# Decoding the weights on VectorE alone, reciprocals as a broadcast weight, the seam's hash ahead of its stage

## The chip, the cores and the metric

The kernel runs on one core of a Trainium2 chip. The metric is the device time of one execution in microseconds. The engines are TensorE (PE, with its weight loads PEld), VectorE (DVE), ScalarE (ACT), GpSimd (POOL) and SyncE (SP), which issues most of the DMAs. Each engine works off its own queue in order; semaphores order them against each other.

## The reference, cut to what matters

```python
# q, k, v: (4, 8, 768, 64) f32; proj: (64, 6)
q_bucket = sum(((q @ proj) > 0) * 2**arange(6)); k_bucket likewise
mask   = q_bucket[:, :, :, None] == k_bucket[:, :, None, :]
scores = where(mask, (q @ k.T) / 8, -1e9); scores -= scores.max(-1)
attn   = exp(scores); attn /= attn.sum(-1) + 1e-9
x      = (attn @ v) as (batch, 768, 512)
h      = relu(x @ w_in)                       # (768, 1024) per batch
gate   = sigmoid(conv3 along the sequence of h with conv_w)
out    = (h * gate) @ w_out                   # (768, 512) per batch
```

The three weights of the second part arrive as 64-bit floats. Each is made on the chip into two parts, high and low, that TensorE can multiply.

## The kernel before, in words

**Units.** Two heads of a batch are a pair; there are 16 pairs. A unit is one head's 128 query rows against all 768 keys; a pair has 12 units, and 192 units are counted through by `i` in the main loop. For unit `i` the loop issues, in this order: the products (line 286, four matmuls into PSUM tile `s`), the maximum (line 299, VectorE, which also moves `s` to `e` in SBUF), the transposes of unit `i-3` (line 329, six) and their copy to `at` (line 336, ScalarE), and the exponential of unit `i` (line 306, ScalarE). `s`, `t` and the hash share a ring of three PSUM tiles, so TensorE can be about one unit ahead of VectorE.

**Bursts.** Two row blocks of two heads, four units, are one step of the values. In every fourth unit (`i` = 3, 7, 11, ...) TensorE gets a block of 14 more matmuls: two that spread the reciprocals of the sums (line 350, transposes of `rec`), and twelve that multiply by `v` (line 355). This unit is called a burst here. In the next one ScalarE copies the spread factors to `rs`; in the next burst VectorE multiplies by them (line 364), and GpSimd splits the product into `xh` and `xl` (lines 365, 366). This holds for the first six pairs. The later ones (`late`, from pair 6 on) divide `e` itself on GpSimd (line 314).

**Decoding.** Lines 87 to 140 decode 16 blocks of weights, 128x512 each: the size of the upper word on ScalarE (87), a clamp on GpSimd (90), four operations on VectorE (95, 97, 102, 104), a cast on ScalarE (136) and two operations on GpSimd (139, 140). This is a generator, `split_weights`, in which the stages of successive blocks overlap. From unit 7 on each burst moves it by `RATE` = 3.75 steps (line 527), a step being mostly one VectorE operation; the feed-forward stage moves it by two steps an iteration. The cast waits for the block's last VectorE operation, since the result lies where the raw block lay.

**The next pair.** Its rows `R` (q and k of two heads, 768 KB) are loaded in the pair before the last (line 191, issued by SP in the pair's unit 7, once nothing reads `R` any more). In units 1 to 7 of a pair the generator `prepare` (line 231) makes the next pair's operands: split of the first head (`hi`, line 204, and in place the rest, line 209), hash (line 219: matmuls of `R` with the projections; line 222: bits on VectorE; 224: their weights on GpSimd), split of the second head. Each part is moved to its partitions by DMAs of SP: 192 KB moves of `hi` and `R`, eight small ones of the bits.

**Stages.** After the first units of pairs 6, 10 and 14 and at the end comes the feed-forward stage of a batch, `ffn`: 16 column blocks through `hidden` (lines 393 to 412) and `output` (423). The place where the loop enters it, in the third unit of a pair, is called the seam. At the seam `prepare` has made two of its seven steps; the rest, the hash among them, come in iterations 3 to 7 of the stage.

Of the kernel before, what the change touches and what calls it, by code (L numbers as in the profile page):

```python
# [28 lines left out]
F32_MAX = 2.0 ** 127 * (2.0 - 2.0 ** -23)  # L29
# [9 lines left out]
RATE = 3.75  # L39
# [4 lines left out]
def lsh_attention_conv_ffn(ctx, tc, qk, v, hw, w_in, conv_w, w_out, consts, ident_in, out):  # L44
# [23 lines left out]

    Q2s = [cp.tile([96, 2, S], F32R, name=f"q2_{i}") for i in range(2)]
# [4 lines left out]
    class Decode:  # L74
# [4 lines left out]
        def __init__(self, raw, n, name):  # L79
            pr, self.name = raw.rearrange("p (n two) -> p n two", two=2), name  # L80
            self.lo, self.hi = pr[:, :, 0].bitcast(U32), pr[:, :, 1]
            self.up, self.low = (ring(wp, bufs, [P, WC], I32, f"w{x}", f"w{x}{name}")[:, :n]
                                for x, bufs in (("u", 2), ("l", 5)))
# [15 lines left out]

        def lower(self):  # L100
            V, up, low = nc.vector, self.up, self.low
# [3 lines left out]
            yield  # L105

    def split_weights():

        todo, ends = [], None

        def ahead():
            if fetched:
                raw, name = fetched.pop(0)
                todo.append(Decode(raw, WC, name))
                todo[-1].size()

        ahead()  # L120
        ahead()
        yield
        for d in todo:
            d.clamp()
        yield
        while todo:
            d = todo.pop(0)
            ahead()
            yield from d.upper()
            if ends:  # L130
                ends()
            if len(todo) == 2:
                todo[-1].clamp()
            yield from d.lower()
            blk = weights[d.name] = cp.tile([P, 2, WC], F32R, tag=f"w{d.name}", name=f"w{d.name}")
            nc.scalar.copy(blk[:, 0, :], d.upf)

            def ends(d=d, blk=blk):
# [38 lines left out]
    class Pair:  # L177
# [53 lines left out]
        def prepare(self):  # L231

            sa, sb, hs = self.split(0), self.split(1), self.hash()
            for now in ((sa,), (), (hs, sa), (hs,), (sb,), (), (sb,)):
                for g in now:
                    next(g, None)
# [362 lines left out]
```

## Time and profile before

| | |
|---|---|
| time, three runs | 748.12, 752.3, 996.83 us; median 752.3 |
| the profiled execution | 750.76 us |
| its span, first to last instruction | 749.0 us |
| mean granted clock of TensorE | 0.984 of full speed |
| PE busy | 714.4 us (95%) |
| DVE busy | 499.2 us (67%) |
| ACT busy | 509.2 us (68%) |
| POOL busy | 373.6 us (50%) |
| share of PE in the chain that ended last | 69% |

The run of 996.83 us stands far from the two others. Busy shares are means over stages with different limits; the stages lie at 0 to 205 us (pairs 0 to 5 and the decoding), 205 to 278 (first feed-forward stage), then 105 us of attention, a stage of some 70 us, and so on. Clock shares are of 2.4 GHz; the lower level is 1.2 GHz.

### The profile page before, as it was taken

The page shows a single profiled execution, that of the slowest core. Times are in us where ns is not written, and L with a number is a line of the kernel's source. Part 1 is how long each engine was busy: PE and PEld are TensorE (multiplying, and loading weights), DVE is VectorE, ACT ScalarE, POOL GpSimd, SP SyncE. Part 2 cuts the span into 40 slices and gives each one's busy share as a digit, 9 for nine tenths or more (in the row PEclk, how much of TensorE's full clock was granted, in tenths as well). Part 3 has the DMA queues.
Part 4 walks back from the last instruction along what each step waited for, and adds up shares of the span by engine and source line. Part 5 has one row for each costly group of instructions (what it writes and reads, how often), then busy time and mean ns, then how long its engine had stood idle before and what let it go on. Part 6 is the DMA issues. An engine that isn't in the chain of part 4 may idle for free.

```text
span 749.0 us, 13385 instructions
## 1 busy us (share of the span) xinstructions
PE 714.4 (95%) x4588; PEld 587.5 (78%) x4588; DVE 499.2 (67%) x1195; ACT 509.2 (68%) x954; POOL 373.6 (50%) x372
## 2 busy tenths in 40 slices
PE   5989999988899999999999999999999999999997
PEld 3767777776679987777788988777788897778986
DVE  7588999977667656666657655665666665564663
ACT  5867887886655548778774557787785547785554
POOL 4366777756566324755735423656645323341221
PEclk8999999998999999999999999999999999999999
DMA  3876576553412102365441302255461211000011
GB/s 141 198 204 155 141 206 181 168 162 85 114 43 72 64 37 70 82 181 136 121 121 31 104 1 105 68 150 132 119 163 33 70 43 63 2 1 1 0 43 43
DMA packets 30357, 72.18 MB, mean 96 GB/s; under 512 B 5937, under 2 KB 7505, under 8 KB 30289
## 3 DMA queue, kind: packets, MB, share of 16 engines
q1 hardware_dynamic: 27696, 62.88, 30.9%
q10 hardware_dynamic: 2592, 8.44, 3.6%
q8 instruction: 37, 0.61, 0.3%
q14 instruction: 32, 0.25, 0.1%
HBM read 27.40 MB, written 6.29 MB: 45 GB/s over the span
## 4 chain that ended last, share of the span: by engine, by line
PE 69%; DVE 4%; POOL 4%; DMA 3%; ACT 1%; issue 1%; SPq 0%; POOLq 0%; DVEq 0%
PE o L423 18%; PE h L393 17%; PE s L286 11%; PE t L329 11%; PE v L355 11%; DVE e L299 2%; DMA k<-R 1%; DMA R<-in_qk 1%; PE hash L219 1%; POOL wuo L139 1%; POOL e L314 1%; POOL wo L140 1%; ACT e L306 1%; DVE wuo L97 1%; POOL R L209 1%
## 5 line engine op out<-in xcount | busy, mean ns | idle before, releaser
L299 DVE TENSOR_SCALAR_CACHE_REDUCE e<-s 128x768 f32<-128x768 f32 x192 | 183.3, 955 | 80.9 <-PE s L286 72.1
L306 ACT ACTIVATE e<-e,st 128x768 f32<-128x768 f32 x192 | 181.2, 944 | 23.1 <-DVE st L303 12.8
L336 ACT COPY at<-t 128x768 f32<-128x768 f32 x192 | 152.3, 794 | 47.3 <-PE t L329 47.1
L329 PE MATMUL t<-ident,e 128*128 128x128 f32 x1152 | 164.5, 280 | 19.9 <-DVE e L299 17.9
L314 POOL TENSOR_SCALAR e<-e,st 128x768 f32<-128x768 f32 x120 | 109.3, 911 | 117.3 <-ACT at L336 59.9
L329 PEld LDWEIGHTS t<-ident,e 128*128 128x128 f32 x1152 | 133.4, 144 | 42.6 <-DVE e L299 22.4
L402 DVE SCALAR_TENSOR_TENSOR ht<-ht,cw 128x384 f32<-128x384 f32 (+1 forms) x128 | 117.8, 921 | 70.0 <-ACT ht L400 66.8
L412 POOL TENSOR_TENSOR g<-ht,g 128x384 fp32r<-128x384 f32 x64 | 72.0, 1125 | 163.9 <-ACT g L411 129.7
L423 PE MATMUL o<-wo,g 128*128 128x512 f32 x576 | 143.3, 395 | 0.7 <-POOL g L412 0.7
L393 PE MATMUL h<-xh,wi 128*128 128x386 f32 x512 | 142.0, 340 | 0.0
L355 PE MATMUL v<-at,v 128*64 128x256 f32 x1152 | 134.9, 383 | 0.0
L423 PEld LDWEIGHTS o<-wo,g 128*128 128x128 f32 x576 | 107.0, 188 | 23.5 <-ACT ht L400 1.2
L286 PE MATMUL s<-K,Q 128*128 128x384 f32 x384 | 118.7, 391 | 1.0 <-POOL K L253 0.9
L355 PEld LDWEIGHTS v<-at,v 128*64 128x64 f32 x1152 | 78.7, 137 | 45.5 <-issue 10.9
L286 PE MATMUL s<-k,q 96*128 96x384 f32 x384 | 102.2, 348 | 2.2 <-DVE e L299 2.2
L405 ACT ACTIVATE ht<-ht 128x384 f32<-128x384 f32 x64 | 33.6, 525 | 96.4 <-DVE ht L402 96.4
L393 PEld LDWEIGHTS h<-xh,wi 128*128 128x128 f32 x512 | 94.0, 188 | 3.7 <-ACT ht L400 1.2
L393 PE MATMUL h<-xl,wi 128*128 128x386 f32 x256 | 86.8, 339 | 0.0
L286 PEld LDWEIGHTS s<-K,Q 128*128 128x128 f32 x384 | 60.1, 196 | 22.2 <-issue 17.4
L286 PEld LDWEIGHTS s<-k,q 96*128 96x128 f32 x384 | 72.9, 197 | 3.0 <-ACT q L266 3.0
L406 DVE TENSOR_TENSOR ht<-ht 128x384 f32<-128x384 f32 x64 | 41.5, 649 | 31.5 <-ACT ht L405 31.3
L209 POOL TENSOR_TENSOR R<-R,hi 128x768 fp32r<-128x768 f32 x30 | 60.4, 2014 | 0.9 <-PE hash L219 0.8
(75 smaller groups left out, 622.2 us busy)
## 6 DMA issues: line engine op xcount, KB each, us to landing
R<-in_qk SPq DMA_DIRECT2D x15, 768.0 KB
K<-hi SPq DMA_DIRECT2D x60, 192.0 KB
v<-in_v SPq DMA_DIRECT2D x16, 384.0 KB
out<-osb SPq DMA_DIRECT2D x24, 256.0 KB
Q<-hi SPq DMA_DIRECT2D x30, 192.0 KB
q<-hi SPq DMA_DIRECT2D x30, 192.0 KB
Q<-R SPq DMA_DIRECT2D x30, 192.0 KB
k<-R SPq DMA_DIRECT2D x30, 192.0 KB
```

The costliest lines, as they stand in the source:

```text
L209: nc.gpsimd.tensor_tensor(lo, R, hi.bitcast(F32), ALU.subtract)
L286: nc.tensor.matmul(self.sp[:, half, :HS], A[:, h, qs], C[:, h, half * HS:(half + 1) * HS], start=(kk == 0), stop=(kk == 1))
L299: nc.vector.tensor_scalar(self.e.rearrange("p (a b) -> p a b", a=2), self.sp[:, :, :HS], MASKED, None, ALU.max, ALU.max, accum_out=self.st ...
L306: nc.scalar.activation(self.e, self.e, AF.Exp, bias=self.st[:, 1:2], scale=SCALE, accum_out=self.sum)
L314: nc.gpsimd.tensor_scalar(self.e, self.e, self.st[:, 3:4], 0.0, ALU.mult, ALU.add)
L329: nc.tensor.transpose(self.tp[:, c // 3, c % 3 * P:(c % 3 + 1) * P], self.e[:, c * P:(c + 1) * P], ident)
L336: nc.scalar.copy(pr.at[self.h][:, :, :, self.tq * P:(self.tq + 1) * P], self.tp[:, :, :3 * P].rearrange("p j (c q) -> p j c q", c=3))
L355: nc.tensor.matmul(av[h * D:(h + 1) * D, :QB], vt[:, c, h, :], ats[h][:, c // 3, c % 3, :], start=(c == 0), stop=(c == NCK - 1), tile_posi ...
L393: nc.tensor.matmul(hp[:, :HW], w, x[:, c0:c0 + HW], start=(n == 0), stop=(n == 3 * NCC - 1))
L402: nc.vector.scalar_tensor_tensor(t[:, a:z], ht[:, o + k - 1 + a:o + k - 1 + z], cw[:, f, k:k + 1], t[:, a:z], ALU.mult, ALU.add)
L412: nc.gpsimd.tensor_tensor(g[:, 1, :], t, g[:, 0, :].bitcast(F32), ALU.subtract)
L423: nc.tensor.matmul(op, l, r, start=(f == 0 and n == 0), stop=(f == NFC - 1 and n == 2))
```

## The change

- **Decoding.** ScalarE's size and GpSimd's clamp go. VectorE does a bitwise and, a maximum, and the old four operations, six in a row, then ScalarE's cast and GpSimd's two operations follow at once; blocks no longer overlap in the generator. `RATE` is 6, less one in a pair's unit 3. Nothing is decoded in the feed-forward stages. `low` and `up` share one ring of four buffers with `bits` and `osb`.
- **Sums.** Three fixed tiles hold 1e-9 in every second column, written once; the exponential's sum goes into the other, and a `tensor_reduce` adds both. The reciprocals are spread on TensorE: four matmuls whose weight is one column, read 64 times, against the identity. GpSimd's spread (line 323) goes.
- **Order.** The product with the factors is made in place in `rs` (two buffers). GpSimd's split of it comes after the decoding of the burst. `prepare` is two generators: the hash in units 3 and 4 ahead of the values, and the splits behind the decoding. In the four units before a seam the hash's generator is moved twice a unit.

```diff
-RATE = 3.75
+RATE = 6.0
+    sums4 = [cp.tile([P, 2 * QB // P, 2], F32, name=f"sums{i}") for i in range(3)]
+    for t in sums4:
+        nc.gpsimd.memset(t, 1e-9)
...
-        def size(self):
-            nc.scalar.activation(self.lowf, self.hi.bitcast(F32), AF.Abs)
-        def clamp(self):
-            nc.gpsimd.tensor_scalar(self.lowf, self.lowf, F32_MAX, F64_MIN, ALU.min, ALU.max)
-        def upper(self):
+        def vector(self):
             V, up, low = nc.vector, self.up, self.low
+            V.tensor_scalar(low, self.hi, 0x7FFFFFFF, None, ALU.bitwise_and)
+            yield
+            V.tensor_scalar(self.lowf, self.lowf, F64_MIN, None, ALU.max)
+            yield
             V.tensor_scalar(low, low, 3, 0x3FFFFFFF, ALU.logical_shift_left, ALU.bitwise_and)
             yield
             V.scalar_tensor_tensor(up, self.hi, -0x40000000, low, ALU.bitwise_and, ALU.bitwise_or)
             yield
...
+        while fetched:
+            raw, name = fetched.pop(0)
+            d = Decode(raw, WC, name)
+            yield from d.vector()
+            blk = weights[name] = cp.tile([P, 2, WC], F32R, tag=f"w{name}", name=f"w{name}")
             nc.scalar.copy(blk[:, 0, :], d.upf)
+            nc.gpsimd.tensor_tensor(d.upf, d.upf, blk[:, 0, :].bitcast(F32), ALU.subtract)
+            nc.gpsimd.tensor_tensor(blk[:, 1, :], d.upf, d.lowf, ALU.add)
+            yield
...
-            for now in ((sa,), (), (hs, sa), (hs,), (sb,), (), (sb,)):
+            return steps((None, None, hs, hs)), steps((sa, None, sa, None, sb, None, sb))
...
-            nc.vector.tensor_scalar(sums, sums, 1e-9, None, ALU.add)
-            nc.vector.reciprocal(sums, sums)
-            nc.gpsimd.tensor_scalar(pr.rec, sums.unsqueeze(3).to_broadcast([P, QB // P, 2, D]), 1.0, 0.0,
-                                    ALU.mult, ALU.add)
+            nc.vector.tensor_reduce(pr.inv, self.sums, mybir.AxisListType.X, ALU.add)
+            nc.vector.reciprocal(pr.inv, pr.inv)
...
-                nc.tensor.transpose(av[:, QB + t * P:QB + (t + 1) * P],
-                                    rec[:, t].rearrange("p h d -> p (h d)"), ident)
+                for h in range(2):
+                    nc.tensor.matmul(av[h * D:(h + 1) * D, QB + t * P:QB + (t + 1) * P],
+                                     inv[:, 2 * t + h:2 * t + h + 1].to_broadcast([P, D]), ident,
+                                     start=True, stop=True, tile_position=(0, h * D))
...
-            fetch(1)
             background(1)
             if i >= 3:
-                next(prep[0], None)
+                prepare(0)
+                prepare(1)
...
-            background(1)
...
-        next(prep[0], None)
+        prepare(0)
+        if ending:
+            prepare(0)
         for _ in range(1 + NCK if ending else AVS[(i - LAG) % 4]):
...
         if burst and i >= W0:
-            background(RATE)
+            background(RATE - (k == PREP + 2))
+        for last in parts:
+            last()
+        prepare(1)
```

Three places show how the instructions move. First VectorE in the burst of unit 27: the multiply, the bits of a hash, decoding, and the next unit's maximum. Before:

```order
L364 TENSOR_TENSOR x_1_1_924<-v_1_1_788,rs_1_1_789 128x256
L222 TENSOR_SCALAR bits_3_933<-hash_3_928,cst 128x384
L95 TENSOR_SCALAR wli_1_583<-wli_1_583 128x512
L97 SCALAR_TENSOR_TENSOR wui_1_582<-rawi_1_456,wli_1_583 128x512
L102 TENSOR_SCALAR wli_1_583<-wui_1_582 128x512
L104 SCALAR_TENSOR_TENSOR wli_1_583<-rawi_1_456,wli_1_583 128x512
L299 TENSOR_SCALAR e_2_2_0_974,st_2_2_0_972<-s_2_2_0_967 128x768
```

What this is after the change (L333 is the multiply, L189 the bits, L101 the last operation of a block, L91 to L99 the first five, L270 the maximum):

```order
L333 TENSOR_TENSOR rs_1_1_786<-v_1_1_785,rs_1_1_786 128x256
L189 TENSOR_SCALAR bits_3_932<-hash_3_927,cst 128x384
L101 SCALAR_TENSOR_TENSOR lowi_1_829<-rawi_1_462,lowi_1_829 128x512
L91 TENSOR_SCALAR lowi_1_955<-rawi_1_586 128x512
L93 TENSOR_SCALAR lowi_1_955<-lowi_1_955 128x512
L95 TENSOR_SCALAR lowi_1_955<-lowi_1_955 128x512
L97 SCALAR_TENSOR_TENSOR upi_1_956<-rawi_1_586,lowi_1_955 128x512
L270 TENSOR_SCALAR e_2_2_0_975,st_2_2_0_974<-s_2_2_0_969 128x768
```

The last operation of one block now stands first, and four of the next block follow; before, one whole block stood there. Second, GpSimd around the same burst. Before, the split of x (L365, L366), the rest of R, the two weight operations, a clamp, the bits and the spread:

```order
L365 TENSOR_SCALAR xh_1_663<-x_1_1_924 128x256
L366 TENSOR_TENSOR xl_1_664<-x_1_1_924,xh_1_663 128x256
L209 TENSOR_TENSOR R_3_722<-R_3_722,hi_3_0_878 128x768
L139 TENSOR_TENSOR wui_0_452<-wui_0_452,wi_0_952 128x512
L140 TENSOR_TENSOR wi_0_952<-wui_0_452,wli_0_453 128x512
L90 TENSOR_SCALAR wli_1_955<-wli_1_955 128x512
L224 TENSOR_SCALAR bits_3_933<-bits_3_933,cst 128x384
L323 TENSOR_SCALAR rec_2_1_1_1006<-sums_2_0_0_843 128x256
```

After:

```order
L111 TENSOR_TENSOR upi_1_830<-upi_1_830,wi_1_951 128x512
L112 TENSOR_TENSOR wi_1_951<-upi_1_830,lowi_1_829 128x512
L336 TENSOR_SCALAR xh_1_661<-rs_1_1_786 128x256
L337 TENSOR_TENSOR xl_1_662<-rs_1_1_786,xh_1_661 128x256
L176 TENSOR_TENSOR R_3_721<-R_3_721,hi_3_0_880 128x768
L191 TENSOR_SCALAR bits_3_932<-bits_3_932,cst 128x384
```

The weight operations (L111, L112) are those of the block that this very burst ends, and they stand ahead of x and R. Third, TensorE at the first seam. Before:

```order
L329 MATMUL t_1_4_1_2388<-ident,e_1_4_1_2292 128x128 x6
L286 MATMUL s_2_0_1_2405<-K_2_1866,Q_2_1865 128x384 x2
L286 MATMUL s_2_0_1_2405<-k_0_75,q_0_73 128x384 x2
L329 MATMUL t_1_5_1_2415<-ident,e_1_5_1_2316 128x128 x6
L393 MATMUL h_0_0_2427<-xh_0_282,wi_0_450 128x386
```

After:

```order
L257 MATMUL s_2_0_1_2401<-K_2_1864,Q_2_1863 128x384 x2
L257 MATMUL s_2_0_1_2401<-k_0_81,q_0_79 128x384 x2
L297 MATMUL t_1_5_1_2411<-ident,e_1_5_1_2310 128x128 x6
L186 MATMUL hash_3_2422<-R_3_2237,hw_sb 32x384 x4
L368 MATMUL h_0_0_2439<-xh_0_285,wi_0_333 128x386
```

The hash, which stood 61 rows further down in the stage, now stands between the last transposes and the first matmul of the stage; the second and third seam are alike.

## Rows read from the trace of the kernel before

**Rows 1.** Windows: window, length, busy us (instructions) per engine, clock, DMA, GB/s.

```profile
62.00:150.00 88.00, 82.11 (x620) 64.33 (x618) 81.98 (x173) 70.78 (x133) 68.99 (x70) 1.00 0.65 180
150.00:204.00 54.00, 45.91 (x312) 37.06 (x308) 37.77 (x85) 36.25 (x67) 32.07 (x33) 0.91 0.46 125
286.00:380.00 94.00, 93.69 (x712) 73.14 (x708) 59.36 (x227) 73.91 (x140) 55.39 (x58) 1.00 0.44 113
```

**Rows 2.** Timeline of VectorE, units 27 to 31: start, us, engine, line, operation.

```profile
79.49 0.42 DVE L364 TENSOR_TENSOR x<-v,rs 128x256 f32<-128x256 f32 x1
...
82.20 1.95 DVE L102 TENSOR_SCALAR wli<-wui 128x512 int32<-128x512 int32 x1
...
85.77 0.94 DVE L299 TENSOR_SCALAR_CACHE_REDUCE e<-s 128x768 f32<-128x768 f32 x1
...
90.84 0.42 DVE L364 TENSOR_TENSOR x<-v,rs 128x256 f32<-128x256 f32 x1
```

**Rows 3.** Timeline of GpSimd in the burst of unit 27.

```profile
81.47 2.40 POOL L209 TENSOR_TENSOR R<-R,hi 128x768 fp32r<-128x768 f32 x1
```

**Rows 4.** VectorE by line: count, duration ns minimum/median/maximum, first and last start.

```profile
L95 DVE TENSOR_SCALAR wli<-wli x8: 417/827/2060, 29.8 to 110.5; 128x512 int32<-128x512 int32 x8
L97 DVE SCALAR_TENSOR_TENSOR wui<-rawi,wli x8: 681/868/2120, 37.9 to 111.4; 128x512 int32<-128x512 int32 x8
L320 DVE TENSOR_SCALAR sums<-sums x18: 157/160/570, 22.4 to 204.3; 128x4 f32<-128x4 f32 x18
```

**Rows 5.** Timeline of VectorE: bursts of units 19, 51, 67 and 71.

```profile
60.99 0.42 DVE L364 TENSOR_TENSOR x<-v,rs 128x256 f32<-128x256 f32 x1
...
138.96 0.42 DVE L364 TENSOR_TENSOR x<-v,rs 128x256 f32<-128x256 f32 x1
...
183.98 0.41 DVE L364 TENSOR_TENSOR x<-v,rs 128x256 f32<-128x256 f32 x1
...
197.99 0.87 DVE L102 TENSOR_SCALAR wlo<-wuo 128x512 int32<-128x512 int32 x1
```

**Rows 6.** Timeline of TensorE after two waits, in brackets the idle time before.

```profile
86.78 0.88 PE L329 MATMUL t<-ident,e 128*128 128x128 f32 x6 [1.54 <-DVE e L299]
...
192.35 0.87 PE L329 MATMUL t<-ident,e 128*128 128x128 f32 x6 [3.54 <-DVE e L299]
...
194.31 1.48 PE L329 MATMUL t<-ident,e 128*128 128x128 f32 x6
```

**Rows 7.** Timelines of SP, TensorE and GpSimd at the second seam, then the first.

```profile
377.76 0.39 SPq L191 DMA_DIRECT2D R<-in_qk  x1
380.28 0.42 PE L393 MATMUL h<-xh,wi 128*128 128x386 f32 x1
382.43 0.83 POOL L204 TENSOR_SCALAR hi<-R 128x768 fp32r<-128x768 f32 x1 [1.44 <-DMA R<-in_qk]
...
186.12 2.00 POOL L209 TENSOR_TENSOR R<-R,hi 128x768 fp32r<-128x768 f32 x1
192.23 0.38 SPq L191 DMA_DIRECT2D R<-in_qk  x1
204.92 0.43 PE L393 MATMUL h<-xh,wi 128*128 128x386 f32 x1
```

**Rows 8.** Timeline of TensorE, the hash in unit 15.

```profile
46.96 0.85 PE L219 MATMUL hash<-R,hw_sb 128*32 128x384 f32 x8 [1.02 <-DMA R<-in_qk]
```

**Rows 9.** Timeline of TensorE: spreads of units 55 and 59.

```profile
148.63 0.39 PE L350 MATMUL v<-ident,rec 128*128 128x128 f32 x2
...
157.28 0.38 PE L350 MATMUL v<-ident,rec 128*128 128x128 f32 x2
```

**Rows 10.** Groups by line: ScalarE's cast, busy us, mean ns, idle before.

```profile
L136 ACT CAST wi<-wui 128x512 fp32r<-128x512 f32 x8 | 4.9, 617 | 7.9 <-DVE wli L104 7.9
```

**Rows 11.** Waits: us in total, times, longest.

```profile
DVE wuo L97 <- POOL wo L140: 8.0, 3, 4.3
```

**Rows 12.** Timeline of GpSimd: a weight operation.

```profile
188.08 1.28 POOL L139 TENSOR_TENSOR wuo<-wuo,wo 128x512 f32<-128x512 f32 x1
```

More of the change, by code (lines that the diff above doesn't have):

```diff
@@ L104, in lower, with split_weights @@
             V.scalar_tensor_tensor(self.lowf, self.lo, 2.0 ** -52, self.lowf, ALU.mult, ALU.mult)
-            yield
[L107 to L138, printed above, removed]
-                nc.gpsimd.tensor_tensor(d.upf, d.upf, blk[:, 0, :].bitcast(F32), ALU.subtract)
-                nc.gpsimd.tensor_tensor(blk[:, 1, :], d.upf, d.lowf, ALU.add)
-        ends()
+    def split_weights():
+        while fetched:
[3 more added lines that the diff above has]
+            blk = weights[name] = cp.tile([P, 2, WC], F32R, tag=f"w{name}", name=f"w{name}")
+            nc.scalar.copy(blk[:, 0, :], d.upf)
+            nc.gpsimd.tensor_tensor(d.upf, d.upf, blk[:, 0, :].bitcast(F32), ALU.subtract)
+            nc.gpsimd.tensor_tensor(blk[:, 1, :], d.upf, d.lowf, ALU.add)
+            yield
     def decode_taps(raw):
         d = Decode(raw, NFC * 3, "cw")
-        d.size()
+        yield from d.vector()
         yield
-        d.clamp()
-        yield
-        yield from d.upper()
-        yield from d.lower()
         nc.vector.tensor_tensor(cw.rearrange("p f k -> p (f k)"), d.upf, d.lowf, ALU.add)
@@ L233, in prepare, with steps @@
             sa, sb, hs = self.split(0), self.split(1), self.hash()
-            for now in ((sa,), (), (hs, sa), (hs,), (sb,), (), (sb,)):
-                for g in now:
-                    next(g, None)
-                yield
+            def steps(plan):
+                for g in plan:
+                    if g:
+                        next(g, None)
+                    yield
+            return steps((None, None, hs, hs)), steps((sa, None, sa, None, sb, None, sb))
         def prepare_now(self):
@@ L293, in maximum @@
             if self.tq == 0 and self.h == 0 and not pr.late:
[L294 removed]
+                pr.sums = sums4[self.qb % 3]
             self.sums = None if pr.late else pr.sums
[L296 removed]
+            self.sum = self.st[:, 2:3] if pr.late else pr.sums[:, 2 * self.tq + self.h, 0:1]
             e = wp.tile([P, 776], F32, tag="e", name=f"e{self.nm}", bufs=EB)
@@ L376, in values, with prepare @@
         if pr.late:
-            return chunks, (out_high, out_low)
-        rs = ring(wp, 1, [P, QB], F32, "rs", f"rs{pr.nm}_{qb}")
-        return [spread, *chunks], (factors, out)
-    g2, prep = [None], [iter(())]
+            return chunks, (out_high, out_low, lambda: None)
+        rs = ring(wp, 2, [P, QB], F32, "rs", f"rs{pr.nm}_{qb}")
+        return [spread, *chunks], (factors, out, parts)
+    g2, prep = [None], [iter(()), iter(())]
+    def prepare(part):
+        next(prep[part], None)
     def hidden(b, half, f, xs):
@@ L484, in lsh_attention_conv_ffn @@
         burst = AVS[(i - LAG) % 4] > 0
-        for high, low in outs:
+        for high, low, part in outs:
             high()
@@ L492, in lsh_attention_conv_ffn @@
         if ending:
-            for high, low in lows:
+            for high, low, part in lows:
                 low()
+                part()
             lows = []
@@ L511, in lsh_attention_conv_ffn @@
             next(first, None)
+        parts = []
         if burst:
-            for high, low in lows:
+            for high, low, part in lows:
                 low()
+                parts.append(part)
             lows = []
         if u and k == PREP and pi + 1 < len(pairs):
-            prep[0] = pairs[pi + 1].prepare()
-        next(prep[0], None)
+            prep[:] = pairs[pi + 1].prepare()
+        prepare(0)
+        if ending:
+            prepare(0)
         for _ in range(1 + NCK if ending else AVS[(i - LAG) % 4]):
```

35 lines of the change are left out of this document (14 added, 21 removed).

## The prediction

> **What bounds the kernel now.** I read the windows first [rows 1]. From 286 to 380 us TensorE is busy 93.69 of 94.00 us and VectorE 59.36: that part, like the feed-forward stages, is bound by TensorE. From 62 to 150 us VectorE is busy 81.98 of 88.00 us, and from 150 to 204 us the mean clock is 0.91: while weights are decoded (units 7 to 71), VectorE decides. So the change can win at most in the first 205 us, and can lose anywhere.
>
> Then I read VectorE's own order in one burst, unit 27 [rows 2]. T0 is the start of the multiply behind a unit's maximum, S1 the next unit's maximum. T0 is 79.49, S1 85.77, and the next burst's T0 90.84. So a period of four units is a burst B = 6.28 us, and 5.07 us for four maxima and the sums; a burst without work beside it leaves TensorE's own period. L102 lasts 1.95 us there, though such an operation (one input, dense) needs 0.42 us at best and one with two inputs 0.68 [rows 4]. GpSimd's row tells why [rows 3]: its L209 ends at 81.47 + 2.40 = 83.87, L102 at 84.15, 0.28 later. A VectorE operation that starts while GpSimd works waits for GpSimd's whole operation, then runs.
>
> That lock is what the Trainium skill (SBUF — State Buffer, "Who interferes with whom") states, with one exception: tensor_reduce never contends on trn2. The sum takes this in below.
>
> **Parts that I cost at nothing.** ScalarE's 16 sizes, GpSimd's 16 clamps and 18 reciprocal spreads go; neither engine ends a wait that bounds, except where GpSimd locks VectorE, which is counted in the bursts. The three memsets of the sums run before GpSimd has any data. The spread becomes four matmuls with 64 columns of weights, two side by side, for two transposes that take 0.38 us together [rows 9]. Between nothing and 0.38 us more, 18 times, that is 0 to 6.8 us of TensorE, beside periods that VectorE bounds: I take 0; where that cover is thin (the five periods of the third stretch below) it could cost 1.9. The split of x leaves the front of GpSimd's queue; nobody needs it before the feed-forward stage.
>
> **The sums.** tensor_reduce takes the place of L320. No trace shows it; L320 lasts 157 to 570 ns [rows 4], so a saving of 0.41 us down to a loss of 0.41 us each, 18 times: from -7.4 to +7.4 us. I take 0, since most of L320 is at the low end (median 160) and the new operation reads as little. By the skill's exception it would last the free 0.16 us always, and the sum would be lower only by what holds some of the L320 now.
>
> **The decode.** Before, a burst has 3 or 4 operations, and GpSimd starts at once on x, R and an older block. Now it has 6 (5 in a pair's first burst), and GpSimd's weight operations wait for the block's last operation and ScalarE's cast, 0.62 us [rows 10]. Free, six cost 4 x 0.42 + 2 x 0.68 = 3.04, with the gaps between starts 3.4 us; with the multiply (0.42) B = 3.8. But the shortened bursts let the blocks drift: in unit 19 the first operation ends a block. GpSimd then starts at T0 + 1.1 + 0.65 = 1.8, and the operations after it wait for L139 (1.28 free [rows 12]), L140 (alike) and the split of x, one by one: B = 6.2 for units 19 and 23, 6.15 for 27 (five operations and the bits), 6.2 for 31 and 35; with the last operation deeper in the burst 5.4, 5.5, 5.5 for 39, 43, 47; 4.6, 4.5, 4.5 for 51, 55, 59; 4.0 and 3.85 for 63 and 67. From each I take 0.15, as operations start faster one behind the other than I laid them out.
>
> Three stretches, T0 from [rows 5] (197.99 is the first decode operation of unit 71, whose multiply is elsewhere):
> - To unit 19. The hash of unit 15 waits for R at 46.96 already [rows 8], so shorter bursts before it gain nothing. After it one operation fewer is held, 1.0 us, and TensorE's wait behind that burst goes, with a clock loss like those below, taken as 1.5 us: **-2.5**.
> - Units 19 to 51, eight periods: before 138.96 - 60.99 = 77.97. After, 8 x 5.07 + 47.15 - 8 x 0.15 = 86.5: **+8.5**.
> - Units 51 to 71, five periods: before 197.99 - 138.96 = 59.03, 8.0 of it waits of L97 for GpSimd's older blocks [rows 11], and the low clock behind them. After, 21.45 + 5 x 5.07 - 0.75 = 46.0; the period of unit 63 would fall under TensorE's own, 157.28 - 148.63 = 8.65 [rows 9] and 0.85 for the hash, so 46.6: **-12.4**.
>
> **The clock.** After a wait of 1.54 us TensorE goes on at full speed; after one of 3.54 us six transposes take 1.48 us, near twice the 0.88 [rows 6], so at the lower level of the granted clock, 1.2 GHz. From 150 to 204 us the mean of 0.91 [rows 1] means 0.09 x 54 = 4.9 us lost; three waits lie in it, those behind L97's three [rows 11], so 1.6 us each.
>
> **The seam.** Where a feed-forward stage begins, the hash of the next pair now stands ahead of the stage's first matmul, and TensorE is in order: every matmul of the stage is queued behind it, and on VectorE the stage's first work behind the bits of this hash. The hash needs R. Before the second stage, R is issued at 377.76 and lands at 382.43, where GpSimd's split starts on it, while TensorE begins the stage at 380.28 [rows 7]. Nothing in the change makes this R earlier: its load waits for the moves out of R, behind bits and splits that keep their places on SP. So TensorE idles 2.15 us, and I take the lower clock after it: bounds 0 (as after 1.54) and 1.6, value 1.6, since the idle time is past the longest after which the clock held. The hash's own 0.85 us only moves. Third stage alike: 2 x (2.15 + 1.6) = **+7.5**. The fourth has no next pair.
>
> At the first stage, R is issued at 192.23, so lands near 196.9, 8.0 us before 204.92 [rows 7]. Now L209 of unit 67 stands behind the weights and x on GpSimd: T0 + 7.8 instead of 186.12 - 183.98 = 2.1, 5.7 later; and 67 to 71 shrinks from 197.99 - 183.98 = 14.0 to 8.8. So 8.0 - 5.7 - 5.2 = -2.9: a wait of 2.9, with 1.6 for the clock: **+4.5**. That this stage loses the decoding beside it, I count as nothing: TensorE covers it; without cover it would give back the little that this stage lost to it.
>
> **Sum.** -2.5 + 8.5 - 12.4 + 7.5 + 4.5 = +5.6 us on the profiled execution's 750.76 us (span 749.0, so 1.8 around it): **756**. The runs' median is 752.3, with 748.12 below, so the profile stands for them within 0.3%.
>
> **Rivals.**
> - *GpSimd does not collide.* If it starts late enough that the bursts of 19 to 51 are free (B = 3.6), those eight periods fall to TensorE's 9.0 (8.65, and a hash in every third), 72 instead of 86.5: 741; R then becomes the limit soon after. For it: GpSimd's wait behind the cast. Against it: the drift.
> - *The seam waits do not show*, because R lands earlier or the clock stays: 756 less 12.0, 744. Both together: 729. Against it: the load's wait is on SP's order, untouched.
> - *VectorE is only loaded more.* The old bursts keep their collisions, and two operations more of 0.5 us each, start to start, come to all 16 blocks: +16; the waits for older blocks in units 59 to 67, 8 us, go; seams +12.0: **771**, slower. It decides from the point where most bursts pass unit 27's 6.28 us, since TensorE's wait then passes the 1.54 us behind which the clock still held [rows 6]. For it: VectorE's 93% busy share from 62 to 150 us while ScalarE has room. The Trainium skill says as much (Perfetto Trace Analysis, "Optimizing Scalar/DVE Operations"): with VectorE saturated, work should go to ScalarE, and this change does the reverse. The trace agrees on the saturation only [rows 1]; against the rival stands that most of the old bursts is waiting, not work.
> - *It only shuffles.* Collisions and waits cancel, and R lands in time at the seams by a hair: 751.
>
> **Chances.** Forecast, 748 to 764: 0.48. No collisions 0.15, no seam waits 0.10, both 0.07, more load 0.12, shuffle 0.08. The range from 739 to 770 takes in the uncollided and the waitless case, the spread's 1.9 and most of the sums' bounds, and leaves out the joint case, half of the loaded one and the tails, about 2 in 10. A measurement of this kernel tells about 2% (15 us) from no change. Below 737: the joint case and half of the uncollided one with the sums at their best, 0.15. Above 767: most of the loaded case and the tail of the forecast, 0.12. Within: 0.73.
>
> **What would show it.** Right: in the profile after, a TensorE wait of 2 us or more on R at the hash ahead of the second and third stage, and a lower clock behind it; held operations in the bursts of 19 to 47, six free ones in about 3.4 us at 11 and 63 to 67; unit 71 some 7 us earlier. Wrong: no wait at the hash; bursts of 19 to 47 near 3.8 us; more clock losses before 205 us than the five of before.

## The result and the profile after

The changed kernel takes 745.1 us (median of 20 runs, 741.95 to 750.48) against 750.2 for the kernel before in the same comparison (20 runs, of which the one of 996.83 us stands apart and is left out of the ratio): ratio **0.9934, 95% interval 0.9915 to 0.9953**, 5 us less. The forecast was 756, 5.6 us more than the profiled execution before. The profiled execution after took 749.26, 4 us above its median (span 747.5), so a second one of the same kernel (746.15, span 744.3; run "again" below) is read beside it.

First the windows of the changed kernel, with the columns of [rows 1].

```profile
62.00:150.00 88.00, 82.56 (x638) 65.69 (x638) 74.74 (x181) 65.01 (x120) 50.04 (x50) 0.96 0.60 166
150.00:204.00 54.00, 46.95 (x370) 36.90 (x367) 41.94 (x110) 39.56 (x74) 31.59 (x34) 0.97 0.52 136
286.00:380.00 94.00, 92.85 (x704) 72.33 (x702) 60.26 (x229) 74.26 (x139) 56.05 (x58) 1.00 0.46 119
```

VectorE, which got two operations a block more, is busy 7 us less from 62 to 150 us than in [rows 1] (78.05, so 4 less, in the second profile, which got further in that window): its busy time holds the time in which it was held by GpSimd. All its decoding of the 16 blocks went from 65.4 us in 64 operations to 62.1 us in 96. Now the burst of unit 23: VectorE, ScalarE and GpSimd in the same stretch.

```profile
67.59 0.42 DVE L333 TENSOR_TENSOR rs<-v,rs 128x256 f32<-128x256 f32 x1
67.92 0.68 DVE L101 SCALAR_TENSOR_TENSOR lowi<-rawi,lowi 128x512 f32<-128x512 uint32 x1
68.52 0.44 DVE L91 TENSOR_SCALAR lowi<-rawi 128x512 int32<-128x512 int32 x1
...
69.91 0.69 DVE L97 SCALAR_TENSOR_TENSOR upi<-rawi,lowi 128x512 int32<-128x512 int32 x1
70.64 1.40 DVE L99 TENSOR_SCALAR lowi<-upi 128x512 int32<-128x512 int32 x1
71.96 0.94 DVE L270 TENSOR_SCALAR_CACHE_REDUCE e<-s 128x768 f32<-128x768 f32 x1
```

```profile
67.89 0.79 ACT L304 COPY at<-t 128x768 f32<-128x768 f32 x1
68.57 0.95 ACT L277 ACTIVATE e<-e,st 128x768 f32<-128x768 f32 x1
...
69.50 0.62 ACT L110 CAST wi<-upi 128x512 fp32r<-128x512 f32 x1
```

```profile
70.20 1.56 POOL L111 TENSOR_TENSOR upi<-upi,wi 128x512 f32<-128x512 f32 x1 [3.50 <-ACT wi L110]
71.83 1.34 POOL L112 TENSOR_TENSOR wi<-upi,lowi 128x512 fp32r<-128x512 f32 x1
```

The block is complete at T0 + 1.0 (L101 ends at 68.60), but the cast starts only at T0 + 1.9, since the unit's copy and exponential stand ahead of it on ScalarE. GpSimd begins at T0 + 2.6; by then four of six operations are through and the fifth, L97, has started, and only L99 is held (1.40 us instead of 0.43). B, multiply to next maximum, is 4.37 us. It is much the same in the bursts of units 19 to 35: 4.35, 4.37, 4.59, 4.37, 4.37; forecast were 6.0 to 6.05. In units 27 to 35 the one held operation is L97 (1.65 to 1.67 us instead of 0.69). The eight bursts of units 19 to 47 take 37.2 us in the second profile, against 36.9 before: five or six operations now fit where three or four did, and the bursts are no shorter.

The hashes at the three seams and the stages behind them, and SP's issues of R before the first two (with the move of R's low part ahead of the first); idle time in brackets.

```profile
201.33 1.51 PE L186 MATMUL hash<-R,hw_sb 128*32 128x384 f32 x8 [3.20 <-DMA R<-in_qk]
...
379.27 0.85 PE L186 MATMUL hash<-R,hw_sb 128*32 128x384 f32 x8 [0.92 <-DMA R<-in_qk]
380.05 0.45 PE L368 MATMUL h<-xh,wi 128*128 128x386 f32 x1
...
553.93 0.85 PE L186 MATMUL hash<-R,hw_sb 128*32 128x384 f32 x8 [1.04 <-DMA R<-in_qk]
```

```profile
191.40 0.74 SPq L178 DMA_DIRECT2D Q<-R  x1
...
196.71 0.38 SPq L158 DMA_DIRECT2D R<-in_qk  x1
...
374.58 0.39 SPq L158 DMA_DIRECT2D R<-in_qk  x1
```

The hash starts 4.6 and 4.7 us behind these issues. The waits on R are there, as forecast: 3.20 us at the first seam, with the low clock level behind it (1.51 us for a hash of 0.85), but only 0.92 and 1.04 at the others (1.29 and 1.01 in the second profile, the 1.29 put down to ScalarE's copy), and there the clock holds. Ahead of unit 71 R is waited for too: the hashes of units 15, 51 and 63 wait 2.33, 0.76 and 1.58 us for it. At unit 39 something else was late.

```profile
105.23 1.01 PE L257 MATMUL s<-k,q 96*128 96x384 f32 x2 [2.16 <-DMA k<-R]
106.03 1.48 PE L297 MATMUL t<-ident,e 128*128 128x128 f32 x6
```

A move of R's low part into k, issued at 98.08, took 7.1 us; TensorE's products waited 2.16 for it, and the six transposes behind them took 1.48, at the lower clock level. The period from unit 35 to 39 was 13.71 us.

### The profile page after: what moved, and what is told of

It reads as the page before. It is cut to its first block, busy times and chain, and to the rows that moved or that the text cites. A ratio compares the mean times of both kernels' runs of the same rounds, so it can differ in the third digit from the quotient of the medians.

```text
span 747.5 us, 13565 instructions
## 1 busy us (share of the span) xinstructions
PE 715.8 (96%) x4696; PEld 589.8 (79%) x4696; DVE 493.4 (66%) x1229; ACT 499.3 (67%) x937; POOL 341.8 (46%) x340
## 4 chain that ended last, share of the span: by engine, by line
PE 72%; DMA 12%; POOL 5%; DVE 4%; issue 3%; SPq 2%; ACT 0%; POOLq 0%; DVEq 0%; ACTq 0%
PE h L368 19%; PE o L398 18%; PE v L325 12%; PE s L257 11%; PE t L297 11%; DMA R<-in_qk 6%; DMA k<-R 5%; PE hash L186 2%; DVE e L270 1%; SPq L174 1%; POOL R L176 1%; DMA K<-hi 1%; POOL e L285 1%; POOL hi L171 1%; DMA rawo<-in_w_out 1%
## 5 line engine op out<-in xcount | busy, mean ns | idle before, releaser
L270 DVE TENSOR_SCALAR_CACHE_REDUCE e<-s 128x768 f32<-128x768 f32 x192 | 183.3, 955 | 79.3 <-PE s L257 69.9
L277 ACT ACTIVATE e<-e,st 128x768 f32<-128x768 f32 x192 | 181.2, 944 | 13.1 <-DVE st L274 7.5
L297 PE MATMUL t<-ident,e 128*128 128x128 f32 x1152 | 161.8, 277 | 6.6 <-DVE e L270 4.8
L377 DVE SCALAR_TENSOR_TENSOR ht<-ht,cw 128x384 f32<-128x384 f32 (+1 forms) x128 | 113.4, 886 | 72.6 <-ACT ht L375 70.3
L297 PEld LDWEIGHTS t<-ident,e 128*128 128x128 f32 x1152 | 131.0, 142 | 27.8 <-DVE e L270 8.6
L257 PE MATMUL s<-K,Q 128*128 128x384 f32 x384 | 116.6, 385 | 1.6 <-POOL K L224 0.9
L325 PEld LDWEIGHTS v<-at,v 128*64 128x64 f32 x1152 | 80.6, 138 | 42.5 <-issue 8.4
L257 PE MATMUL s<-k,q 96*128 96x384 f32 x384 | 100.5, 343 | 4.4 <-ACT q L237 2.3
L257 PEld LDWEIGHTS s<-k,q 96*128 96x128 f32 x384 | 71.0, 192 | 5.7 <-ACT q L237 3.1
L176 POOL TENSOR_TENSOR R<-R,hi 128x768 fp32r<-128x768 f32 x30 | 56.9, 1895 | 0.6 <-DVE st L274 0.6
```

Source lines behind the costliest of these rows:

```text
L176: nc.gpsimd.tensor_tensor(lo, R, hi.bitcast(F32), ALU.subtract)
L257: nc.tensor.matmul(self.sp[:, half, :HS], A[:, h, qs], C[:, h, half * HS:(half + 1) * HS], start=(kk == 0), stop=(kk == 1))
L270: nc.vector.tensor_scalar(self.e.rearrange("p (a b) -> p a b", a=2), self.sp[:, :, :HS], MASKED, None, ALU.max, ALU.max, accum_out=self.st ...
L277: nc.scalar.activation(self.e, self.e, AF.Exp, bias=self.st[:, 1:2], scale=SCALE, accum_out=self.sum)
L297: nc.tensor.transpose(self.tp[:, c // 3, c % 3 * P:(c % 3 + 1) * P], self.e[:, c * P:(c + 1) * P], ident)
L325: nc.tensor.matmul(av[h * D:(h + 1) * D, :QB], vt[:, c, h, :], ats[h][:, c // 3, c % 3, :], start=(c == 0), stop=(c == NCK - 1), tile_posi ...
```

## The experiments

All ratios are to the kernel before, timed on the same chip. E1 to E4 ran on one chip, E5 to E8 on another, then E9 to E11, and E12 alone.

**E1, again.** No edit.

> The changed kernel itself, one more profile. In the first profile of it one period near 100 us took 13.7 us instead of 9.45: a move of the low part into k took 7.1 us there, TensorE's products waited 2.2 us for it and the clock fell. Theory: an accident of that execution; here this move lands in 3 to 5 us, that period is about 10.3 (9.45 and the hash), and the span is 743 to 744 instead of 747.5. Rival: the loss belongs to the kernel (the decode's DMAs stand there in every execution); then the same wait stands at 103 to 105 us and the span is 746 to 748. In both, bursts of units 19 to 35 are 4.35 to 4.6 us (multiply to next maximum) with one held VectorE operation.

Measured: 746.15 us (one run), span 744.3. The period from unit 35 to 39 is 9.46 us; the move into k takes 5.3 us (issued at 96.39), a little more than expected, and TensorE does not wait for it. R is issued at 101.70 instead of 105.24, and the hash waits 1.76, so that the period from 39 to 43 is 11.48:

```profile
106.18 0.85 PE L186 MATMUL hash<-R,hw_sb 128*32 128x384 f32 x8 [1.76 <-DMA R<-in_qk]
```

So the loss at 105 us belongs to one execution and not to the kernel (in E3's profile that period is 9.45 as well); the waits of the hash on R stay.

**E2, two buffers for R.**

```
- self.R = ring(wp, 1, [P, 2, S], F32R, "R", ...)
+ self.R = ring(wp, 2, [P, 2, S], F32R, "R", ...)
```

> The changed kernel with two buffers for R instead of one: the load of R then waits for nothing that the present pair still does. Theory (units 27 to 71 of the changed kernel are bound by the chain of R: moves out of R, load of R, hash): the seven waits of the hash for R, 10.1 us in all, go, with the low clock behind three of them (0.7 to 1.6 us each); periods of 9.45 us (bound by VectorE's bursts of 4.4 and 5.07) take their place: about 10 us less than the changed kernel, 735, ratio to the kernel before near 0.980. Rival 1 (SP's own queue is the bound, since it issues every move and load in order): R comes at most 2 us earlier, ratio 0.990 to 0.994. Rival 2 (VectorE's bursts are the bound already): hash waits turn into waits behind the maximum, ratio 0.993.

Measured: 735.4, ratio 0.9794 (0.9771 to 0.9818), as the theory had it, though 3.3 us of the waits for R remain. TensorE's waits up to 210 us, first of E1, then with two buffers:

```profile
PE hash L186 <- DMA R<-in_qk: 9.5, 6, 3.2
PE t L297 <- DVE e L270: 5.6, 10, 1.5
```

```profile
PE t L297 <- DVE e L270: 5.8, 9, 1.5
...
PE hash L186 <- DMA R<-in_qk: 3.3, 4, 1.1
```

The single buffer of R bounds much of the changed kernel up to the first stage: against E1's profile, unit 71's first decode operation comes 3.9 us earlier (181.44), the first stage 6.8 (192.01), the end 10.0. What is left in units 19 to 35 are VectorE's bursts of 4.35 to 4.6 us, with periods of 9.4 to 9.7.

**E3, the hash back in the stage.** Without the two lines that the main loop got:

```
- if ending:
-     prepare(0)
```

> The changed kernel with one thing undone: the hash ahead of a feed-forward stage goes back into the stage (fourth step of it). Theory: the three waits for R ahead of a stage (3.2, 0.92 and 1.04 us) go, with about 1 us of low clock at the first; the hash itself costs its 0.85 us in either place: 5 to 6 us less, 739 to 740, ratio near 0.986. Rival 1 (the waits only move: GpSimd and SP wait for the same R, and the pair after the stage needs it): as the changed kernel, 0.993. Rival 2 (as predicted blind: each seam worth 3.75, the first 4.5, 12 in all): 733, ratio 0.977.

Measured: 739.1, ratio 0.9854 (0.9815 to 0.9892). The theory holds: against the changed kernel's 0.9934 the seam's part of the change costs 6 us, half of the forecast 12.0.

**E4, GpSimd's x and R ahead of the decode**, as before the change.

```
+ for last in parts: last()
+ prepare(1)
  if burst and i >= W0: background(...)
- for last in parts: last()
- prepare(1)
```

> The changed kernel with one thing undone: within a burst GpSimd's split of x and its split of R stand ahead of the decoding again, as in the kernel before; VectorE's six operations stay. Theory (bursts became short because GpSimd starts late, at T0 + 2.6, when five of six operations are through): GpSimd starts at T0 + 0.45, holds VectorE's operations one by one, bursts of units 19 to 47 are 6 us and more instead of 4.4; R and the bits come 2 to 4 us earlier, so that hash waits fall; 5 to 12 us more than the changed kernel, 750 to 757, ratio 1.000 to 1.009. Rival (what counts is the number of operations, not GpSimd's start): bursts stay at 4.4, and the earlier R gives 4 to 6 us: 740, ratio 0.986.

Measured: 767.8, ratio 1.0221 (1.0192 to 1.0249): the direction of the theory, but some 22 us above the changed kernel where 5 to 12 were expected. The burst of unit 23 here, VectorE, GpSimd and then TensorE behind it:

```profile
72.49 0.41 DVE L333 TENSOR_TENSOR rs<-v,rs 128x256 f32<-128x256 f32 x1
...
74.96 1.38 DVE L95 TENSOR_SCALAR lowi<-lowi 128x512 int32<-128x512 int32 x1
76.38 1.66 DVE L97 SCALAR_TENSOR_TENSOR upi<-rawi,lowi 128x512 int32<-128x512 int32 x1
```

```profile
72.99 0.78 POOL L336 TENSOR_SCALAR xh<-rs 128x256 fp32r<-128x256 f32 x1 [7.26 <-DVE rs L333]
73.85 0.79 POOL L337 TENSOR_TENSOR xl<-rs,xh 128x256 fp32r<-128x256 f32 x1
74.64 1.42 POOL L111 TENSOR_TENSOR upi<-upi,wi 128x512 f32<-128x512 f32 x1
```

```profile
79.93 1.15 PE L297 MATMUL t<-ident,e 128*128 128x128 f32 x6 [2.46 <-DVE e L270]
...
82.16 1.48 PE L297 MATMUL t<-ident,e 128*128 128x128 f32 x6
```

GpSimd starts at T0 + 0.5 and takes the operations one by one; bursts of units 19 to 43 are 6.4 to 7.5 us. TensorE then waits 2.46 us, and the clock falls (0.88 from 62 to 150 us), so that periods are 13.1 to 14.1 instead of B + 5.07, which would be 11.5 to 12.6. The expected size left the clock out.

**E5, the cast ahead of copy and exponential.**

```
+ cast_first = burst and W0 <= i < 74
- w.to_sbuf(); u.exponential()      # ahead of background()
+ w.to_sbuf(); u.exponential()      # behind background(), where cast_first
```

> The changed kernel with one order changed: in the bursts of units 7 to 71 ScalarE does the decode's cast ahead of that unit's copy of the transposes and its exponential, not behind them. Theory (in the changed kernel the cast waits 1.75 us behind that copy and that exponential, so that GpSimd starts at T0 + 2.6, when five of six VectorE operations are through): GpSimd starts at T0 + 1.7 to 1.9, holds three or four operations, and the bursts of units 19 to 35 come to about 6.0 to 6.2 us, as predicted blind, instead of 4.37; less hash waits, 5 to 12 us more than the changed kernel, 750 to 757, ratio 1.00 to 1.01. Rival (GpSimd's start is set by something else, or an earlier start costs nothing): bursts stay near 4.4, ratio 0.993.

Measured: 748.2, ratio 0.9965 (0.9945 to 0.9984). The burst of unit 19 (T0 58.78): ScalarE, GpSimd, VectorE.

```profile
59.82 0.62 ACT L110 CAST wi<-upi 128x512 fp32r<-128x512 f32 x1 [0.64 <-DVE lowi L101]
```

```profile
60.52 1.28 POOL L111 TENSOR_TENSOR upi<-upi,wi 128x512 f32<-128x512 f32 x1 [4.94 <-ACT wi L110]
...
63.19 0.84 POOL L336 TENSOR_SCALAR xh<-rs 128x256 fp32r<-128x256 f32 x1
```

```profile
60.62 1.47 DVE L95 TENSOR_SCALAR lowi<-lowi 128x512 int32<-128x512 int32 x1
62.12 1.65 DVE L97 SCALAR_TENSOR_TENSOR upi<-rawi,lowi 128x512 int32<-128x512 int32 x1
63.81 0.51 DVE L99 TENSOR_SCALAR lowi<-upi 128x512 int32<-128x512 int32 x1
```

GpSimd starts at T0 + 1.74 here and in unit 23, where the forecast had put it (2.2 to 2.4 in units 27 to 35), and bursts of units 19 to 35 grow from some 4.4 us to between 5.4 and 5.6. So the cast's place sets GpSimd's start. But the forecast of 6.2 for such a start was too high: two operations are held, by the two weight operations; the split of x hardly holds the sixth (0.51). The five bursts cost 5.3 us more. The time rose by some 2 us only (0.9965 against 0.9934, with intervals that just overlap), less than the expected 5 to 12: the waits for R up to 210 us fell from 9.5 us (E1) to 1.8. The edit also moves ScalarE's copy back, for which TensorE now waits 4.0 us in nine waits, so the time is not the price of GpSimd's start alone.

**E6, the kernel before with the new reciprocals alone.** Sums, `reciprocals` and `spread` as in the change, all else as before.

> The kernel before with one part of the change: sums and reciprocals (tensor_reduce, reciprocal, spread by matmuls with a broadcast weight; GpSimd's spread of the reciprocals goes). Theory: this part is worth nothing by itself; the spread takes 0.1 to 0.3 us more of TensorE, 18 times, mostly covered; GpSimd's operation that goes (1 us in every fourth unit) may free a held VectorE operation here and there: 750, ratio 0.995 to 1.003. Rival 1 (the gain of the change is here, since GpSimd holds VectorE less): ratio 0.985 to 0.993. Rival 2 (the spread's longer time shows): 754, ratio 1.004 to 1.008.

Measured: 749.4, ratio 0.9977 (0.9957 to 0.9997): nearly nothing.

**E7, two buffers and the hash in the stage** (E2 and E3 together).

> The changed kernel with two buffers for R and with the hash back in the feed-forward stage. With two buffers alone the three hashes ahead of a stage still wait for R, 1.11, 1.26 and 0.26 us. Theory: these 2.6 us go too: 732 to 733, ratio 0.975 to 0.977. Rival (R in time, the place of the hash is indifferent): 735, ratio 0.979.

Measured: 733.1, ratio **0.9776** (0.9756 to 0.9796): the lowest ratio here. It is clearly below E3's; against E2's 0.9794 the intervals overlap, so the times alone do not exclude the rival. In the trace no hash waits ahead of a stage any more, and R is waited for three times, 1.8 us in all (six times, 4.8 us, with two buffers alone).

**E8, GpSimd's work of a burst issued a unit later** on top of E7: weights and x in the next unit, the low part of R in the fourth and eighth unit of a pair instead of the third and seventh. The part of the edit that moves the low part of R (weights and x go through a list that is emptied in the next unit):

```
- return ..., steps((sa, None, sa, None, sb, None, sb))
+ return ..., steps((sa, None, None, sa, sb, None, None, sb))
```

> As the kernel with two buffers and the hash in the stage, and GpSimd's work of a burst (the weights' two operations, the split of x, the low part of R) is issued one unit later, where VectorE has only maxima, which are not held in the traces (a maximum started 0.1 us after a GpSimd operation and took its usual 0.94 us). Theory (the one VectorE operation that GpSimd still holds makes bursts 4.37 instead of 3.6 us): bursts 3.6 to 3.7, periods fall to TensorE's own 8.65 and 0.85 for a hash: 9 to 10 us less than without, 723 to 724, ratio 0.963 to 0.965. Rival 1 (the later low part of R makes TensorE wait at a pair's first units, or the hash): 728 to 733, ratio 0.969 to 0.977. Rival 2 (GpSimd then holds the sums and reciprocals of VectorE instead, and the clock falls): as without or slower.

Measured: 753.2, ratio 1.0029 (0.9998 to 1.0060), a miss. GpSimd's start did not move: its queue was empty, and it starts when the cast is done. Bursts of units 19 to 35 stayed at 4.36 to 4.38 us (one, with the bits, 5.79), and the first stage begins at 189.04, in E7 at 189.11. The time above E7's, some 20 us, is lost behind that: from 286 us on, where GpSimd also normalises `e`, the low part of R now stood ahead of that (from 293.16 to 294.99, for one). TensorE's waits from 286 to 374 us; over the whole span they are 17.6 us, in E7 2.0:

```profile
PE t L306 <- POOL e L294: 7.9, 6, 1.6
```

**E9, the decode of before in the new order.** Operations, buffers and steps of the old decode, 3.75 steps a burst and two an iteration of the stage, as before; the rest as changed.

> The changed kernel with one part undone: the decode of the kernel before (sizes on ScalarE, clamps on GpSimd, four VectorE operations a block, 3.75 steps a burst); reciprocals, hash ahead of the stage, and GpSimd's x and R behind the decode stay. Theory (the order pays only together with the new decode, where GpSimd has nothing ready at a burst's start; with the old one an older block's operations are ready there at once and hold VectorE as before): bursts of 3.5 to 6.5 us as in the kernel before; time = the kernel before, less 1.5 for the reciprocals, plus 6 for the seams: 752 to 758, ratio 1.001 to 1.009. Rival (the order alone pays): bursts near 3.5, 738 to 746, ratio 0.983 to 0.993.

Measured: 745.7, ratio 0.9911 (0.9880 to 0.9942). The theory falls, the rival holds. Unit 31's burst, VectorE and GpSimd:

```profile
87.41 0.42 DVE L99 TENSOR_SCALAR wli<-wli 128x512 int32<-128x512 int32 x1
87.93 0.69 DVE L101 SCALAR_TENSOR_TENSOR wui<-rawi,wli 128x512 int32<-128x512 int32 x1
88.66 0.43 DVE L106 TENSOR_SCALAR wli<-wui 128x512 int32<-128x512 int32 x1
89.11 0.71 DVE L108 SCALAR_TENSOR_TENSOR wli<-rawi,wli 128x512 f32<-128x512 uint32 x1
```

```profile
89.69 1.28 POOL L143 TENSOR_TENSOR wui<-wui,wi 128x512 f32<-128x512 f32 x1 [3.38 <-ACT wi L140]
```

With x and R behind the weights, and the weights waiting for the cast, the old decode's four operations run free too: bursts without bits are 3.65 to 3.9 us in units 19 to 47. Those with bits, 6.4 to 6.8, wait for a hash that waits for R.

**E10, R loaded four units earlier** on top of E7 (`load` at the pair's third unit instead of the seventh).

> The kernel with two buffers for R and the hash in the stage, and the load of R issued four units earlier (third unit of a pair instead of the seventh). Theory (with two buffers the hash still waits 0.6, 0.5 and 0.7 us because SP issues the load late and it takes 7 us): those waits go, periods with a hash fall from 10.2 to 9.5, 2 us less: 731, ratio 0.974. Rival (the earlier load collides with the weights' loads, or stands on SP ahead of moves that are needed sooner): 733 to 737, ratio 0.977 to 0.982.

Measured: 738.1, ratio 0.9809 (0.9775 to 0.9843), the rival's ratio; the interval overlaps E7's, so a loss against E7 is not shown, but the gain did not come. No hash waits for R any more, but three periods at which a pair begins are 11.6, 11.9 and 12.8 us; TensorE's waits there are put down to the move into k (2.1 us in two waits) and to exponentials (3.6 in three). What delays these was not followed further.

**E11, the cast later** on top of E10: cast, weights, x and low part of R behind the next unit's copy `rs`.

> The kernel of the earlier R with the cast issued later: on ScalarE it stands behind the next unit's first copy (rs), and GpSimd's weights, split of x and low part of R behind it. (One unit later on GpSimd alone changed nothing, since GpSimd starts whenever the cast is done.) Theory: the cast starts at T0 + 3.2 instead of T0 + 1.9, GpSimd at T0 + 3.9, after the sixth VectorE operation; bursts fall from 4.37 to 3.6 us, periods from 9.44 to TensorE's own 8.65; over the 13 periods to unit 67 8 to 10 us less than the kernel of the earlier R: 722 to 724, ratio 0.962 to 0.965. Rival 1 (GpSimd's 5.3 us then reach into the next burst and hold its first operations): bursts 4.2 to 5, no gain, 730 to 735. Rival 2 (the later low part of R makes TensorE wait for k or Q): 728 to 740.

Measured: 744.3, ratio 0.9898 (0.9866 to 0.9930). Bursts of 3.66 us as the theory had them (units 19 and 23, periods 8.86 and 8.88), but two periods of 14 us: a miss, slower than E10 and than the theory and both rivals had it.

**E12, the same with R loaded at its old place.**

> As the kernel of the later cast, but with R loaded at its old place, behind the move of the low part (two buffers, hash in the stage): in the kernel of the later cast bursts of 3.66 us stood beside two waits of 3 us at a pair's first units, where the earlier load of R and the moves on SP were in each other's way. Theory (those waits come from the earlier load): bursts of 3.66 to 4.4, no such waits, 4 to 6 us less than two buffers and hash in the stage alone (733.1): 727 to 729, ratio 0.969 to 0.971. Rival (the waits come from the low part of R itself, 1.3 us later on GpSimd): the same waits again, 735 to 744, ratio 0.980 to 0.990.

Measured: 738.3, ratio 0.9841 (0.9825 to 0.9858), the rival again. TensorE at the second head of a pair, and SP's move of the low part:

```profile
101.36 0.59 PE L266 MATMUL s<-K,Q 128*128 128x384 f32 x2 [2.06 <-DMA Q<-R]
102.17 1.01 PE L266 MATMUL s<-k,q 96*128 96x384 f32 x2 [0.22 <-DMA k<-R]
```

```profile
95.36 1.02 SPq L187 DMA_DIRECT2D Q<-R  x1
96.43 1.00 SPq L187 DMA_DIRECT2D k<-R  x1
```

GpSimd has the low part ready at 94.13 (it started at 92.31), SP comes to it at 95.36, behind the bits and the high part, and TensorE gets it 6 us after that. So with shorter bursts the moves out of R are late here. A second wait, 2.95 us at 135.34, is put down to an exponential that had ended 0.9 us before; what ended it was not followed. No kernel here has both the short bursts and moves in time.

## Why the prediction was wrong

| Term, us | forecast | profile after | second profile |
|---|---|---|---|
| to unit 19 | -2.5 | -2.8 | -3.6 |
| 19 to 51 | +8.5 | +3.7 | 0.0 |
| 51 to 71 | -12.4 | -9.4 | -9.1 |
| 71 to the first stage | +4.5 | +6.4 | +6.5 |
| first stage to the end | +7.5 | +0.6 | +1.5 |
| sum | +5.6 | -1.5 | -4.7 |

(The columns are differences to [rows 5, 7] and to the stages' first `h`; after, T0 of units 19 and 51 is 58.15 and 139.82, the first decode operation of unit 71 starts at 189.44, the first stage at 202.77; in the second profile 57.38, 135.36, 185.31, 198.77.) The rows of the profile after:

```profile
58.15 0.41 DVE L333 TENSOR_TENSOR rs<-v,rs 128x256 f32<-128x256 f32 x1
139.82 0.41 DVE L333 TENSOR_TENSOR rs<-v,rs 128x256 f32<-128x256 f32 x1
189.44 1.27 DVE L93 TENSOR_SCALAR lowo<-lowo 128x512 f32<-128x512 f32 x1
202.77 0.69 PE L368 MATMUL h<-xh,wi 128*128 128x386 f32 x1
```

Against the second profile the sum is 10.3 us too high: 8.5 from the bursts, 6.0 from the later seams and 1.1 from the first stretch, less 3.3 and 2.0 that the two other terms missed the other way.

**Failed: "GpSimd then starts at T0 + 1.1 + 0.65 = 1.8"**, and with it the term of +8.5. The cast was given its 0.62 us [rows 10] and no queue; on ScalarE it stands behind a copy of 0.79 and an exponential of 0.95. The eight bursts measure 37.2 us in the second profile instead of 45.95, 8.8 less, and the term missed by 8.5. (The eight values of the forecast add up to 47.35, not 47.15, so its own term would be +8.7.) E5 puts the start back to T0 + 1.74 and gets 1.1 of the 1.7 us by which the bursts were forecast too long, so the rest of the error is "operations wait for L139, L140 and the split of x, one by one": x hardly holds any. In the profile after, the late move at 105 us makes one period 4.3 us longer than in the second, and this is where its +3.7 comes from.

**Mis-sized: the second and third seam, 2 x (2.15 + 1.6).** The waits are 0.92 and 1.04, and the clock holds behind them, as it did in [rows 6] behind 1.54. The sum had put 2.15 for the wait and 1.6 for a clock loss that did not come. "Nothing in the change makes this R earlier" failed by 1.2 us: TensorE would have begun the stage at 378.35 (380.05 less 0.78 for the hash and 0.92), 3.77 after R's issue, against 2.52 in [rows 7]. 1.0 of that is a move of R's low part that landed sooner (3.2 us after its issue ended, 4.1 before); why it did stays open. The hash that is taken out of a stage also comes back: from the third seam, which gets no hash inside its stage, to the fourth it is 1.4 us less, of which the hash itself is 0.85.

**Right in mechanism, and in the number by luck: the first seam.** A wait of 2.9 and a lower clock were forecast; 3.20 and a hash of 1.51 us came. But R's issue came 8.1 us later after T0 of unit 67 than before (196.71 - 180.33 against 8.25) where 5.7 were forecast, since the move of its low part stood on SP until 191.40, behind bits and high part, and landed late; and TensorE was free for the hash only 3.1 us earlier, not 5.2, since unit 71 holds five decode operations where before it held three. The two errors, 2.4 and 2.1, cancel in the wait; the second is why the term is 1.9 too small. E3 confirms the seams' sign with 6 us.

**Right in sign and cause, 3 us too large: 51 to 71.** The waits of L97 for older blocks are gone; the bursts of units 51 and 63 hold waits of 0.76 and 1.58 for R that the sum did not have (1.01 and 1.76 in the second profile). That R then limits was said under the first rival only, and not carried into the sum; E2 shows that it was worth 3.9 us by unit 71, and 10 in all.

**Right: to unit 19.** As forecast, the shorter bursts ahead gained little at the hash of unit 15 (46.35 against 46.96); the rest came behind it.

**Right at nothing:** reciprocals and spread (E6). The spread takes 0.66 us where it took 0.38, near the upper bound, and the cover held. The reduction, all 18 times:

```profile
L291 DVE TENSOR_REDUCE inv<-sums x18: 149/151/153, 23.1 to 197.3; 128x4 f32<-128x8 f32 x18
```

It is never held, where L320 went up to 570 ns [rows 4]; at 186.50 it takes 0.15 us while GpSimd's L112 runs from 186.18 to 187.46. The trace agrees with the exception in the Trainium skill (SBUF — State Buffer, "Who interferes with whom") that the forecast left outside its sum; it is not the only one there, as the prediction has it, but one of several.

**Which part of the change pays.** Three kernels and an estimate set the decode against GpSimd's order. Old decode, old order: 0.9977 (E6), and 0.008 for the seam (E3 against the change) makes an estimate of 1.006. Old decode, new order: 0.9911 (E9). New decode, old order: 1.0221 (E4). Both new: 0.9934. So the gain comes from the order, some 11 us with the old decode and 22 with the new; the new decode costs 12 in the old order and nothing that these intervals can tell in the new one. The price of the seam is that of the changed kernel; E9 waits only 0.50 us at its first seam, so the 11 and the 12 are estimates. The rival "VectorE is only loaded more", 771, came near what E4 measures, 767.8, partly by luck: its condition (bursts past 6.28 us) is met there, but its 12.0 for the seams are 6 by E3. In the changed kernel that condition fell away with the order alone. Among the rivals "The seam waits do not show", 744, was nearest to the measured 745.1, and that is luck: the waits show and cost 6 us. In mechanism "GpSimd does not collide", 741, was nearest; it collides once a burst instead of never. "GpSimd's wait behind the cast" stood there for it; its length was not worked out.

## What to carry to other kernels

When one engine holds another, work out the start of the holder's first instruction through every in-order queue that feeds it; here 0.9 us in ScalarE's queue were worth 5 us of bursts, of which some 2 showed in the time (E5). An instruction in front of a queue that must wait (weights behind a cast) can be worth more than ready work there, since it keeps the engine from starting into another's series; and issuing it later does nothing while that wait is what sets its start (E8). After a stretch gets shorter, look for the single buffer whose reload then bounds: a second buffer of R, and the seam undone, gave 12 us more than the change itself.

## What the runs showed of the hardware

A held VectorE operation starts at its usual place and is only longer, so that its busy share contains waiting: in unit 23 L99 takes 1.40 us instead of 0.43 and ends at 72.04, 0.28 behind GpSimd's L111.

VectorE's maxima (0.93 to 0.96 us, 192 times), multiplies (0.41 to 0.43, 18 times) and bits (0.62), which read PSUM, are not held in the profile after: in unit 23 the maximum starts 0.13 us after GpSimd's L112 and takes its usual 0.94; in unit 31 the multiply from PSUM starts at 86.75, while GpSimd's L171 runs from 86.36 to 87.20, and takes 0.41. The prediction's rule, that a VectorE operation that starts while GpSimd works waits for it, is too wide by these and by the reduction.

The lock also works the other way: GpSimd's L336, 0.40 to 0.41 us in most bursts, takes 0.84 where it starts while VectorE's L97 still runs (E5, 63.19 against 62.12 + 1.65).

The clock held behind waits of 0.92, 1.04 and 1.76 us. It was at the lower level for six transposes (1.48 us) behind a wait of 2.16 and for a hash (1.51) behind one of 3.20, and a hash behind one of 2.33 took 1.30, in part at either level. The length of the wait alone does not decide it: in E11 TensorE waits 2.37 us for Q at 169.17 and goes on at full speed (clock 1.00 from 169 to 174 us).

The same move of R's low part, 192 KB, landed 3.0 us (issued at 67.23, R's load freed at 70.25) to 7.1 us after its issue. What else was under way then was not compared.
